# Block-causal attention and a two-layer product on one core: batch 0's second half in float32, two chunks of 192 to a bank, identity inside the plan, and work that may go to more than one engine

## The chip, the cores and the metric

The kernel runs on one core of a Trainium2 chip. The core has a matrix engine (TensorE, PE in the profile; PEld are its weight loads), a vector engine (DVE), an activation engine (ACT), a general engine (GpSimd, POOL) and a queue that issues transfers (SyncE, SP). The metric is the device time of one execution in microseconds, as the median of several runs. Before the change it is 1071.83 us (three runs, 1071.18 to 1075.56).

## What is computed

`q`, `k` and `v` are 8 batches x 8 heads x 576 positions x 64, in float32. Each head does softmax attention in which a block of 64 positions sees itself and the blocks before it. The heads' outputs, put side by side, are 4608 rows of 512, and these go through two products with `h * tanh(softplus(h))` (Mish) between them:

```python
scores = scale * np.matmul(q, k.transpose(0, 1, 3, 2))
mask = block_i >= block_j
scores = np.where(mask, scores, -1000000000.0)
scores = scores - np.max(scores, axis=-1, keepdims=True)
attn = np.exp(scores)
attn = attn / (np.sum(attn, axis=-1, keepdims=True) + 1e-09)
...
h = x @ w_in            # 512 x 2048
g = h * np.tanh(sp)     # sp is softplus(h)
return (g @ w_out)      # 2048 x 512
```

The weights reach the kernel as 64-bit words, which it turns into float32 itself.

## The kernel before

**Numbers.** A float32 value is scaled by a power of two and held as two float16 parts, high and low; a product is then three float16 products (high-high, high-low, low-high). Where the kernel calls a pair of heads "own" or "wide", it skips the split and multiplies float32 as it is.

**Units of work.** A batch has four pairs of heads and two halves of its queries: `HALVES` are positions 0 to 384 and 384 to 576. A `Tile` is one half of one batch; it has 384 or 192 columns.

- `load_pair` (line 733) brings a pair's queries and keys in. Own pairs (batch 0, half 0) read float32 straight into buffers laid over `Et` (`firsts`, lines 351 to 367). All others load into the single tiles `ql` and `kl`, square and sum them (line 811, ACT), reduce across partitions on POOL (line 819), work out scales on DVE (lines 451, 461 and 824), round to the high part `xh` (line 842 on ACT or 849 on DVE), take the remainder `xl` (line 857, DVE), and copy the parts crosswise into a set `QA`, `QB`, `KA`, `KB` by twelve transfers (line 876). There are two such sets. The first nine pairs (`WIDE = 9`) keep the values `V` in float32; later ones split them (lines 892 to 903).
- `attend` (line 934) does one head and one half: the score product A (line 954, from `KA` and `QA`) into one of two PSUM tiles `ss`; the column maximum over key chunks (lines 979 and 992, into `mt`); its maximum over partitions by an all-reduce on POOL (line 1021, into `mr`); minus that maximum into a row of `QB` (line 1028 on DVE or 1035 on ACT); the second score product B (line 954 again, from `KB` and `QB`), which adds the row and the low-order part; the exponential (line 1046, ACT, needs a table); a memset on POOL that hides masked blocks (line 1057); high and low parts of the result (lines 1064 or 1069, and 1075); the value product `u` (line 1092 in float32; 1103 to 1105 as three float16 products); the division by the sum (lines 1126 to 1152); and its two halves `xt_hi` (1163 or 1168) and `xt_lo` (1171). There is one PSUM tile for `u`.
- `weight` (line 489) turns one quarter of a weight matrix into float32 (lines 528 and 545, DVE), sums its squares (556, ACT; 564, POOL), rounds it to the high part (578 on ACT or 585 on DVE) and makes the low part, for three quarters of `w_in` on PE with a scaled identity (596 to 619).
- `Tile.turn` (1194) transposes `xt_hi` and `xt_lo` by transfers; `m1` (1217) is the first product with the Mish activation (1262, ACT, another table than the exponential's); `split` (1278) makes high and low parts of the result; `m2` (1316) is the second product, its evacuation (1357 or 1364) and the store. `m1` and `m2` use a ring of three PSUM tiles `acc`.

**The order.** Nothing is issued as it is written. Each step is put into a `Plan` (line 122) with its engine, an estimated time, what it comes after, and the rings of buffers it takes and frees. `Plan.order` (251) runs a small simulation of the five queues, forward and backward in turns (`go`, line 160), from due times in the table `DUE`; each simulated engine that is free takes the ready step with the earliest due time. The order of the best round is emitted, and each engine executes its own list in that order. A step given with `other=` may run on a second engine, and the simulation takes the one that is free:

```python
for e in o.ways:
    ready[e].append((due[i], i))
```

Steps that are outside the plan come first: memsets, mostly on POOL (lines 350 to 442), and the identity (line 478, on POOL) with its negative (479, on ACT).

Of the kernel before, what the change touches and what calls it, by code (L numbers as in the profile page):

```python
# [19 lines left out]
P = 128  # L20
D = 64
EPS = 1e-9
# [7 lines left out]
    "w": ((198, 45.5, 93.5, 196.5), (118, 220.5, 212.5, 283)),  # L30
    "batch": (209, 220, 278.5, 419.5, 570, 584.5, 680, 822.5),
    "load": (
        (68, 178.5, 94, 89.5),
        (30.5, 24, 165.5, 75.5),
        (143, 130.5, 114.5, 381.5),
        (249, 231.5, 537, 626),
        (450, 465, 506, 532),
        (588, 502.5, 635.5, 628.5),
        (601, 778.5, 735, 673.5),
        (770, 742, 753.5, 656.5),  # L40
        (1259, 954, 806.5, 722.5),
    ),
    "tile": (
        (-10, 235, 68, 43, 118, 37, 41.5, 27.5,
         62.5, 140, 114, 81, 57, 122, 242.5,
         124, 242.5, 120, 204.5, 123.5, 192, 191.5),
        (183.5, 167.5, 87, 61, 129, 80.5, 91, 168.5,
         187.5, 187.5, 115, 163, 265.5, 268.5, 150,
         152, 228.5, 207, 210, 253, 206, 251),
        (103, 130, 155, 132.5, 215, 161, 223.5, 254,  # L50
         188, 203, 201, 270, 399.5, 239.5, 212,
         236, 333.5, 253, 340.5, 375.5, 275.5, 297),
        (253, 168.5, 125.5, 198.5, 289.5, 223, 331.5, 201.5,
         270.5, 394, 316, 368, 286, 369, 296.5,
         511, 308, 562.5, 417.5, 301.5, 373.5, 497.5),
        (232, 318.5, 267, 318, 322.5, 342.5, 487, 377.5,
         415.5, 371.5, 407.5, 319.5, 372.5, 377, 435,
         367.5, 415.5, 399.5, 433, 405.5, 368, 381),
        (328.5, 234, 438.5, 423, 666.5, 634.5, 798.5, 750.5,
         354, 429, 449.5, 442.5, 669.5, 602.5, 621,  # L60
         451.5, 411, 455.5, 533, 469, 648, 604.5),
        (474, 527, 530.5, 473, 536.5, 440, 425.5, 417.5,
         444, 541, 539.5, 524, 546.5, 716, 589,
         645, 449, 529.5, 520, 558, 710, 554),
        (380.5, 532.5, 342.5, 384, 451.5, 504.5, 630.5, 609,
         554, 495.5, 586.5, 512, 660.5, 538, 660.5,
         526, 612.5, 544.5, 692.5, 752.5, 760.5, 719),
        (481, 516, 610, 701.5, 676, 702, 588, 666.5,
         622, 748.5, 705, 739.5, 812.5, 655.5, 692,
         758, 790.5, 750.5, 855, 753.5, 751.5, 828.5),  # L70
        (683.5, 611.5, 574, 555.5, 764.5, 884.5, 506.5, 776,
         585, 615, 733.5, 611.5, 700.5, 680, 625,
         723, 945.5, 630.5, 737, 824, 666, 700),
        (585, 586, 612, 666.5, 620, 811.5, 578, 809,
         599.5, 541, 612.5, 626.5, 682.5, 781, 569.5,
         668.5, 655, 724.5, 657.5, 594.5, 814, 665),
        (781, 620.5, 638, 598.5, 699, 685, 692, 535,
         744.5, 796, 710, 762, 990.5, 631.5, 568,
         884, 869.5, 886, 735.5, 917, 1007, 823),
        (638.5, 1084.5, 660.5, 1071.5, 884, 798.5, 888.5, 766.5,  # L80
         586.5, 780.5, 618, 585, 843.5, 643.5, 933.5,
         766, 646.5, 875, 595, 775.5, 807, 983),
        (736.5, 605, 640.5, 609.5, 734.5, 726.5, 837, 818.5,
         882.5, 881, 857.5, 741, 963, 902, 1124.5,
         1161.5, 996, 738, 735, 794, 766, 751.5),
        (797, 835, 1111, 713.5, 806, 783.5, 943, 780.5,
         868.5, 936, 874.5, 882.5, 849.5, 863, 1069.5,
         1038, 1039, 975.5, 930, 958, 1087.5, 817.5),
        (779, 851, 790, 618.5, 759.5, 896, 933, 783,
         853, 997.5, 1080, 949, 1101, 1129, 1002.5,  # L90
         1131.5, 1065, 950, 955, 943, 989.5, 784.5),
# [30 lines left out]
class Plan:  # L122
# [7 lines left out]
    LAT, LATPE, OWN = 0.15, 0.2, 0.06  # L130
# [10 lines left out]

    def part(self, kind, *at):
# [5 lines left out]
    def add(self, eng, us, emit, after=(), take=(), free=(), other=None, table=None):  # L148
        self.ops.append(Op(eng, us, emit, after, take, free, self.due, other))
        self.ops[-1].table = table  # L150
        return self.ops[-1]

    def lat(self, a, b):
        if a.eng == "sp":
            return self.BEGIN + a.work + self.DONE
        if a.eng != b.eng or len(a.ways) > 1 or len(b.ways) > 1:
            return self.LATPE if a.eng == "pe" else self.LAT
        return 0.0 if a.eng == "pe" else self.OWN

    def go(self, due, back=False):  # L160
# [14 lines left out]
        while events:  # L175
            now = events[0][0]
            while events and events[0][0] <= now:
# [11 lines left out]
                for x in getattr(o, after):  # L189
                    j = x.i  # L190
                    lat = self.lat(x, o) if back else self.lat(o, x) * (o.eng != "sp")
# [59 lines left out]
    def order(self):  # L251
# [6 lines left out]
        _, end, _ = self.go([o.due for o in ops])  # L258
        best = None
        for _ in range(self.ROUNDS):  # L260
# [23 lines left out]
def products(ns, full=False, rows=128):  # L284

    if full:
        return sum(n / 600 + 0.07 - min(n, 320) / 9000 for n in ns), sum(n * rows / 32 for n in ns)
# [11 lines left out]
def pool(n):  # L299
    return 0.4 + n / 230  # L300
# [8 lines left out]
def attention_moe(  # L309
# [44 lines left out]
    for i in range(NP):  # L354
# [8 lines left out]
        nc.gpsimd.memset(m["KF"][D:P, 0], 0.0)  # L363
        nc.gpsimd.memset(m["KF"][0:D, 1], 0.0)
        for j in (0, P + 1):
            nc.gpsimd.memset(m["VF"][:, :, j : j + 1], 1.0)
        firsts.append(m)
    sets = []
    for i in range(2):
        shapes = {  # L370
            "QA": [P, 2, S],
            "QB": [D + 1, 2, S],
            "KA": [P, 2, KW],
# [5 lines left out]
        for nm, t in (  # L379
# [7 lines left out]
        nc.gpsimd.memset(m["KB"][0:D, :, S:KW], 0.0)  # L387
        for j in (0, P + 1):
            nc.gpsimd.memset(m["VF"][:, :, j : j + 1], 1.0)
        nc.gpsimd.memset(m["VF"][64:P, 4, 1 : 1 + P], 0.0)  # L390
# [26 lines left out]
    dv, tt = room(2, "dv", [P, 6]), room(2, "tt", [P, 3, D])  # L417
    ql, kl = room(1, "ql", [P, S])[0], room(1, "kl", [P, S])[0]
# [22 lines left out]
    for t in pe[1], p_hi[1], p_lo[1]:  # L441
        nc.gpsimd.memset(t[:, 896:1024], 0.0)
# [26 lines left out]


# [7 lines left out]
    make_identity(nc, ident)  # L478
    nc.scalar.mul(minus, ident, -1.0)
# [9 lines left out]
    def weight(which, wait, room_free):  # L489
# [11 lines left out]
        last = [None] * len(raws)  # L501
        done = []
        for g in range(NG):
# [6 lines left out]
            for r in range(0, nrow, per):  # L510
# [12 lines left out]
                    [last[i]] + wait,  # L523
# [26 lines left out]
                last[i] = a  # L550
# [31 lines left out]
                other=(  # L582
# [5 lines left out]
                ),  # L588
            )
            if g < PEW[which]:  # L590
# [8 lines left out]
                    [sc] + scaled[-2],  # L599
# [52 lines left out]
    def batch(b):  # L652
# [38 lines left out]
        new["sx"] = add("dve", 0.6, scale_x, [red])  # L691

# [36 lines left out]
    WIDE = 9  # L729
# [762 lines left out]
```

## Time and profile before

| | |
|---|---|
| median of three runs | 1071.83 us |
| the profiled execution | 1073.09 us |
| its span, first to last instruction | 1071.3 us |
| mean granted TensorE clock | 0.971 |
| matmul records of lines 1237 and 1331 (`m1` and `m2`) | 6144 of 9958 |
| activation tables changed | 173 times, 1283 ns each |
| all-reduces of the maximum on POOL | 128, mean 1567 ns |

A group's row has its line, engine, operation, what it writes and reads, shapes and count; then busy time in microseconds and the mean of one in nanoseconds; then the idle time of that engine just before, and what ended it. In a timeline the first number is the start in microseconds and the second the duration; a bracket at the end has the idle time before it. "issue" as the cause of a wait means that the profile shows nothing that the engine waited for. A row of waits has the total in microseconds, how many times, and the longest. Matmuls are pipelined, so their recorded durations overlap: what one costs is read from the distance between starts. Some matmul records can be missing.

### The profile page before, as it was taken

The numbers are of one execution on the slowest core, as the hardware profiler recorded it, in microseconds if no ns is written. First come the engines' busy times: TensorE is split into PE (matmuls) and PEld (weight loads), VectorE is DVE, ScalarE is ACT, GpSimd is POOL, SyncE is SP. The second block draws the span as 40 slices with busy tenths as digits, with TensorE's granted clock in tenths as the row PEclk, the third lists the DMA queues.
The fourth block names the chain that finished last, engine by engine and source line by source line (L and its number), as shares of the span: only waits on it lengthen the run. The fifth ranks groups of instructions, "written<-read, shape, count | busy, mean of one in ns | idle before, by whom it ended". The sixth has DMA issues, their size and how long they took to land. (4 is left out here: it accounts for less than half of the span.)

```text
span 1071.3 us, 25657 instructions
## 1 busy us (share of the span) xinstructions
PE 1009.7 (94%) x9958; PEld 766.2 (72%) x9958; DVE 739.8 (69%) x1872; ACT 771.2 (72%) x1239; POOL 268.7 (25%) x410
## 2 busy tenths in 40 slices
PE   2888989989999999999999999999999998999998
PEld 1466767777776687777767687677778686767778
DVE  3888888785987578757885678746887578833500
ACT  2557887766988679867877789758887688735521
POOL 4242332241232033312431122212332133301000
PEclk7867999999999999999999999999999999999999
DMA  7767643342434433340435233441434342220100
GB/s 253 215 208 185 198 119 86 95 111 77 98 78 110 107 72 77 106 110 25 105 100 128 64 74 96 113 102 28 105 91 110 91 94 71 50 45 8 31 15 23
DMA packets 126200, 103.78 MB, mean 97 GB/s; under 512 B 51328, under 2 KB 112256, under 8 KB 126080
## 3 DMA queue, kind: packets, MB, share of 16 engines
q1 hardware_dynamic: 126080, 102.16, 36.5%
q8 instruction: 78, 1.28, 0.5%
q14 instruction: 42, 0.34, 0.1%
HBM read 56.10 MB, written 9.44 MB: 61 GB/s over the span
## 5 line engine op out<-in xcount | busy, mean ns | idle before, releaser
L1331 PE MATMUL acc<-Gt,wo_h 128*128 128x192 f16 (+1 forms) x2048 | 385.8, 287 | 1.9 <-ACT Et L1262 1.1
L1237 PE MATMUL acc<-x_lo,wi_h 128*128 128x192 f16 (+1 forms) x1024 | 295.0, 288 | 3.2 <-DMA x_lo<-xt_lo 3.2
L1237 PE MATMUL acc<-x_hi,wi_h 128*128 128x192 f16 (+1 forms) x1024 | 295.1, 288 | 2.0 <-ACT Et L1262 1.3
L1237 PE MATMUL acc<-x_hi,wi_l 128*128 128x192 f16 (+1 forms) x1024 | 295.0, 288 | 0.0
L1331 PE MATMUL acc<-Gt,wo_l 128*128 128x192 f16 (+1 forms) x1024 | 293.8, 287 | 0.0
L1021 POOL PARTITION_ALL_REDUCE mr<-mt x128 | 199.6, 1567 | 300.9 <-DVE mt L992 265.6
L1237 PEld LDWEIGHTS <-wi_h 128*128 128x128 f16 x2048 | 192.2, 98 | 77.4 <-issue 10.6
L1331 PEld LDWEIGHTS <-wo_h 128*128 128x128 f16 x2048 | 188.2, 98 | 51.2 <-issue 1.8
L1262 ACT ACTIVATE Et<-acc,bv 128x384 f32<-128x384 f32 (+1 forms) x256 | 125.5, 498 | 91.0 <-PE acc L1237 89.1
L992 DVE TENSOR_TENSOR mt<-mt,ss 128x192 f32<-128x192 f32 (+3 forms) x448 | 127.6, 297 | 13.6 <-ACT mt L979 9.2
L1304 DVE SCALAR_TENSOR_TENSOR Gt<-Et,bv,Gt 128x1536 f16<-128x1536 f32 (+1 forms) x64 | 91.5, 1431 | 54.2 <-ACT Gt L1291 54.0
L1331 PEld LDWEIGHTS <-wo_l 128*128 128x128 f16 x1024 | 100.0, 98 | 34.5 <-issue 1.3
L1237 PEld LDWEIGHTS <-wi_l 128*128 128x128 f16 x1024 | 100.4, 98 | 33.7 <-issue 1.2
L1046 ACT ACT_TABLE_LOAD x86 | 110.3, 1283 | 18.6 <-PE ss L954 8.2
L1046 ACT ACTIVATE pe<-ss,pv 128x768 f32<-128x768 f32 (+1 forms) x120 | 113.2, 956 | 7.9 <-PE ss L954 5.4
L1075 DVE TENSOR_TENSOR p_lo<-pe,p_hi 128x768 f16<-128x768 f32 (+1 forms) x108 | 113.4, 1051 | 4.5 <-ACT p_hi L1064 3.5
L1057 POOL MEMSET pe<- 64x64 f32 (+1 forms) x192 | 34.4, 210 | 318.1 <-ACT pe L1046 287.1
L1262 ACT ACT_TABLE_LOAD x87 | 111.6, 1283 | 1.5
L954 PE MATMUL ss<-QB,KB 65*128 65x192 f16 (+5 forms) x512 | 67.0, 254 | 29.9 <-POOL pv L819 13.0
L1103 PE MATMUL u<-V,p_hi 128*128 128x65 f16 x810 | 85.4, 194 | 2.1 <-DVE tt L1152 2.1
L1105 PE MATMUL u<-V,p_lo 128*128 128x65 f16 x810 | 84.7, 194 | 0.8 <-DVE p_lo L1075 0.6
L1104 PE MATMUL u<-V,p_hi 128*128 128x64 f16 x810 | 85.3, 193 | 0.0
(107 smaller groups left out, 1391.0 us busy)
## 6 DMA issues: line engine op xcount, KB each, us to landing
VL<-in_v_dram SPq DMA_DIRECT2D x32, 288.0 KB, 3.3
kl<-in_k_dram SPq DMA_DIRECT2D x32, 288.0 KB, 3.2
wo_l<-in_w_in_dram SPq DMA_DIRECT2D x8, 1024.0 KB, 5.7
Gt<-in_w_out_dram SPq DMA_DIRECT2D x16, 512.0 KB, 4.0
ql<-in_q_dram SPq DMA_DIRECT2D x28, 288.0 KB, 3.4
QA<-xh SPq DMA_DIRECT2D x112, 72.0 KB, 2.2
VL<-in_v_dram SPq DMA_DIRECT2D x27, 256.0 KB, 3.0
out_dram<-ot SPq DMA_DIRECT2D x32, 192.0 KB, 2.1
```

Source lines behind the costliest of these rows:

```text
L954: nc.tensor.matmul(ss[:, col : col + q1 - qs], lhsT=k_, rhs=q_, start=x == 0 and col % 512 == 0, stop=True, skip_group_check=True,)
L992: nc.vector.tensor_max(t, t, sv(ss_[A.slot % NSS]))
L1021: lambda: nc.gpsimd.partition_all_reduce(mr[rm][:, 0:n], mt[rm][:, 0:n], P, RED.max),
L1046: lambda: nc.scalar.activation(*spread(pe[rm], ss_[A.slot % NSS]), AF.Exp, scale=st.get("esc", D ** -0.5)),
L1075: lambda: nc.vector.tensor_sub(p_lo[rm][:, 0:W], pe[rm][:, 0:W], p_hi[rm][:, 0:W]),
L1103: nc.tensor.matmul(o, lhsT=h, rhs=vh, start=j == 0 and z == 0, stop=False)
L1104: nc.tensor.matmul(o[:, 0:D], lhsT=h, rhs=vo, start=False, stop=False)
L1105: nc.tensor.matmul(o, lhsT=l, rhs=vh, start=False, stop=end)
L1237: nc.tensor.matmul(pt[:, 0:n], lhsT=w[:, d, f * P : (f + 1) * P], rhs=x[:, d, :], start=d == 0 and z == 0, stop=d == NP - 1 and z == 2,)
L1262: nc.scalar.activation(Et[:, (self.i * NG + g) % NE, j, 0:n], acc_[c.slot % NACC][:, 0:n], AF.Mish, scale=fc[:, 0, g : g + 1])
L1304: lambda g_hi=g_hi, g_lo=g_lo, ev=ev: nc.vector.scalar_tensor_tensor(out=g_lo, in0=ev, scalar=self.s_g, in1=g_hi, op0=ALU.mult, op1=ALU.su ...
L1331: nc.tensor.matmul(pt[:, 0:n], lhsT=w[:, f, o * P : (o + 1) * P], rhs=g, start=f == 0 and z == 0, stop=f == NF - 1 and z == 2,)
```

## The change

- **Batch 0's second half.** `ring_pairs(0, Q0, (1,), True)` now loads its pairs as own ones: queries of 384 to 576 into a part of `ql` or `kl`, keys into `KF`, a float32 view over the memory of `QA` and `KA` (now one tile `QK`), with no scales, splits or crossing transfers. The score product A is then float32. `WIDE` is 8: batch 1's first pair splits its values.
- **Chunks of 192 share a bank.** In tiles of 192 columns (`K = 2`) two chunks of `m1` go to the two halves of one `acc` tile, and one Mish activation reads both; in `m2` two output chunks share a tile and a store, with two evacuation instructions.
- **Two heads share a weighing.** The value products of a pair's two heads for one half go to one `u` tile, which is taken by the first head and freed after the second's; sums, reciprocal, weighting, `xt_hi` and `xt_lo` are then done once for both.
- **Identity in the plan.** It follows batch 0's first all-reduce on POOL.
- **Several possible engines.** `other` is a list, and POOL is a third choice for three kinds of step.
- **Memsets** for the own pairs are merged; those of the sets go to DVE.
- **The planner:** new due times throughout, a slack of 0.7 us ahead of PE steps after batch 0, and other cost figures (`OWN`, `pool`, the float32 products of up to 65 columns, the scales, the row of `QB`).

The diff, cut to its core:

```diff
-        if other:
-            self.ways[other[0]] = other[1:]
+        for way in other:
+            self.ways[way[0]] = way[1:]
...
-            return self.LATPE if a.eng == "pe" else self.LAT
+            return self.LATPE if a.eng == "pe" else self.LAT + b.slack
...
 def pool(n):
-    return 0.4 + n / 230
+    return 0.42 + n / 300
+
+
+def elem(n):
+
+    return 0.2 + n / 700
...
-        nc.gpsimd.memset(m["KB"][D : D + 1], MSC)
-        nc.gpsimd.memset(m["KA"][:, :, S:KW], 0.0)
+        nc.vector.memset(m["KB"][D : D + 1], MSC)
+        nc.vector.memset(m["QK"].bitcast(F32), 0.0)
...
-    make_identity(nc, ident)
-    nc.scalar.mul(minus, ident, -1.0)
...
             hi = add(
                 "act",
                 act(2048) + 0.09,
...
+                ), (
+                    "pool",
+                    elem(2048),
+                    lambda whi=whi, f=f, g=g: nc.gpsimd.tensor_scalar_mul(
+                        whi, f, w_s[:, 0, g : g + 1]
+                    ),
+                )],
...
+        if b == 0:
+            e = add("pool", 0.6, lambda: make_identity(nc, ident), [red])
+            last["unit"] = [
+                e,
+                add("act", act(P), lambda: nc.scalar.mul(minus, ident, -1.0), [e]),
+            ]
...
-    WIDE = 9
+    WIDE = 8
...
-                (m["Q"], qT[b, rows, q0:q1], []),
-                (m["KF"][0:D, 0], kT[b, rows, 0:k1][0:D], []),
-                (m["KF"][D:P, 1], kT[b, rows, 0:k1][D:P], []),
+                (m["Q"], qT[b, rows, q0:q1], wait),
+                (m["KF"][0:D, 0, 0:k1], kT[b, rows, 0:k1][0:D], wait),
+                (m["KF"][D:P, 1, 0:k1], kT[b, rows, 0:k1][D:P], wait),
...
+                ), (
+                    "pool",
+                    elem(n),
+                    lambda j=j, n=n, src=src: nc.gpsimd.tensor_scalar_mul(
+                        xh[j][:, 0:n], src, sc[:, j : j + 1]
+                    ),
+                )],
...
-            [p_in] + st["C"],
-            take=[u_ring],
-        )
+            [p_in] + st["C"] + st["u", half],
+            take=[] if a else [u_ring],
+        )
...
-            lambda: nc.scalar.copy(th, tx),
-            [o] + old,
...
+                ("pool", elem(nqc * P), lambda: nc.gpsimd.tensor_copy(out=th, in_=tx)),
...
+                    Et[:, (self.i * NG + g) % NE, j : j + K, 0:n],
+                    acc_[c.slot % NACC][:, 0 : K * n].rearrange("p (k n) -> p k n", k=K),
...
-    ring_pairs(0, Q0, (1,))
+    ring_pairs(0, Q0, (1,), True)
...
+        plan.slack = SLACK
```

More of the change, by code (lines that the diff above doesn't have):

```diff
@@ L21 @@
 D = 64
+E = D + 1
 EPS = 1e-9
@@ L56 @@
[L56 to L67, printed above, removed]
@@ L146, in part, with add @@
             self.due = self.due[i]
-    def add(self, eng, us, emit, after=(), take=(), free=(), other=None, table=None):
+    def add(self, eng, us, emit, after=(), take=(), free=(), other=(), table=None):
         self.ops.append(Op(eng, us, emit, after, take, free, self.due, other))
         self.ops[-1].table = table
+        self.ops[-1].slack = self.slack * (eng == "pe")
         return self.ops[-1]
@@ L190, in go @@
                     j = x.i
-                    lat = self.lat(x, o) if back else self.lat(o, x) * (o.eng != "sp")
+                    lat = self.lat(x, o) if back else self.lat(o, x)
+                    if o.eng == "sp" and not back:
+                        lat = x.slack
                     at[j] = max(at[j], now + lat)
@@ L257, in order @@
                 o.due = min(o.due, n.due - o.us - self.lat(o, n))
-        _, end, _ = self.go([o.due for o in ops])
+        start, end, engine = self.go([o.due for o in ops])
         best = None
+        if None not in engine:
+            best = max(end), start, end, engine
         for _ in range(self.ROUNDS):
@@ L522, in weight @@
                     ),
-                    [last[i]] + wait,
+                    [used[i]] + wait,
                 )
@@ L1371, in m2, with evac, evac_act @@
-                ev_ = self.evacs
+                ev_ = self.evacs
+                def evac(op, o=o, c=parts[0], e=o // K):
+                    for k in range(K):
+                        cols = slice(k * n, (k + 1) * n)
+                        op(
+                            ot[ev_[e].slot % 2][:, cols],
+                            acc_[c.slot % NACC][:, cols],
+                            fc[:, 1, o + k : o + k + 1],
+                        )
+                def evac_act(evac=evac):
+                    evac(lambda o, i, s: nc.scalar.activation(o, i, AF.Copy, scale=s))
```

460 lines of the change are left out of this document (245 added, 215 removed).

## The prediction

> **What bounds the kernel now.** I read the page's busy shares first, then the busy time by stretches of 25 us, then who waited for whom, then the opening 40 us engine by engine.
>
> ```profile
> span 1071.3 us, 25657 instructions
> ...
> PE 1009.7 (94%) x9958; PEld 766.2 (72%) x9958; DVE 739.8 (69%) x1872; ACT 771.2 (72%) x1239; POOL 268.7 (25%) x410
> ```
>
> ```profile
> 0.00:25.00 25.00, 5.29 (x12) 3.38 (x12) 8.75 (x16) 6.01 (x13) 10.53 (x42) 0.81 0.73 243
> 25.00:50.00 25.00, 21.85 (x69) 11.84 (x69) 22.04 (x49) 14.22 (x31) 9.75 (x15) 0.78 0.67 213
> ...
> 100.00:125.00 25.00, 24.16 (x168) 17.42 (x169) 22.60 (x65) 20.72 (x34) 7.12 (x9) 0.91 0.72 209
> ...
> 275.00:300.00 25.00, 23.99 (x240) 17.53 (x239) 22.37 (x55) 23.16 (x38) 8.90 (x12) 1.00 0.40 96
> ```
>
> The columns after the length are PE, weight loads, DVE, ACT, POOL, the granted clock, DMA share and GB/s. There are two stages. Up to about 100 us PE mostly waits or does little of the product work: 5.3 us in the first 25, and a granted clock of 0.78 in the next. There the vector engine (DVE) is full (22.04 of 25). After that PE sets the pace, 24 of 25 us and more, and after 180 us it loses little; its two longest waits there, in total, times and longest:
>
> ```profile
> PE ss L954 <- ACT QB L1035: 9.3, 10, 1.6
> PE acc L1237 <- DMA x_lo<-xt_lo: 3.2, 5, 0.9
> ```
>
> The first is the second score product waiting for the row of negative maxima (QB), which comes from POOL's all-reduce. So from here on a microsecond that the maximum comes late beyond its slack is a microsecond of PE, because each engine's order is fixed when the program is made.
>
> **The opening.** POOL, ACT and PE in the first 26 us, with the two places where POOL changed its code:
>
> ```profile
> 17.16 0.28 POOL masks.py:199 TENSOR_SCALAR_AFFINE_SELECT p_lo<-p_lo 128x128 f32<-128x128 f32 x1 [7.19 <-issue]
> 23.46 1.44 POOL L1021 PARTITION_ALL_REDUCE mr<-mt  x1 [6.02 <-DVE mt L992]
> ...
> 25.22 1.50 POOL L1021 PARTITION_ALL_REDUCE mr<-mt  x1
> ```
>
> ```profile
> masks.py:199 POOLq MODIFY_POOL_CONFIG  x2: 21/21/21, 10.0 to 10.0; - x2
> ```
>
> ```profile
> L1021 POOLq MODIFY_POOL_CONFIG  x2: 1/1/1, 17.7 to 17.7; - x2
> ```
>
> ```profile
> 20.40 0.27 DVE L992 TENSOR_TENSOR mt<-mt,ss 64x128 f32<-64x128 f32 x1
> ```
>
> ```profile
> 17.48 0.31 ACT L479 ACTIVATE p_lo<-p_lo 128x128 f16<-128x128 f32 x1 [15.46 <-POOL p_lo masks.py:199]
> ```
>
> ```profile
> 25.44 0.80 PE L954 MATMUL ss<-QB,KB 1*128 1x256 f16 x3 [13.03 <-POOL pv L819]
> ```
>
> The select that builds the identity had nothing to wait for, and still POOL was idle for 7.19 us, from a configuration instruction at 10.0 us on. The first all-reduce has its input at 20.67 us (DVE's 20.40 plus 0.27) but starts at 23.46, 6.0 us after the select; a configuration again stands at the head of that gap. The next all-reduce follows without any. I read this as POOL running one set of code at a time: memset needs none, the select got one, the all-reduce another, and each change costs 6.0 to 7.2 us in which POOL does nothing.
>
> The Trainium skill says in its "GPSIMD Engine Reference", section 2.1 "Instruction dispatch", that POOL's kernels are loaded at run time and that the first call to a freshly loaded one pays about 6 us (5.95) that no instruction shows; 6.02 and 7.19 agree with it. It does not say which operations share a set.
>
> **The change, part by part.**
>
> *Identity moved behind the first all-reduce, memsets merged or given to DVE.* ACT no longer stands for 15.46 us before its first copy. One load of all-reduce code remains. PE's 13.03 us wait could shrink by up to about 12, but from 25 us on DVE is full, so the stage gets back only what DVE could not do meanwhile: it ran 8.75 of the first 25 us. The added DVE memsets fit in that idle time; without it they would cost about 4 us, from what POOL needs for the same clearing. If the select needs its own code again, up to 13.2 us go back to the stage. I take -7 (from +1 to -12).
>
> *Batch 0's second half in float32.* It removes for four pairs two squares on ACT, a small all-reduce, the scale arithmetic, two roundings, two remainders on DVE, and twelve crossing DMAs each on SP's queue; loads go straight into the pair sets.
>
> ```profile
> L857 DVE SCALAR_TENSOR_TENSOR xl<-kl,pv,xh 128x576 f16<-128x576 f32 x32 | 25.9, 808 | 0.1
> ```
>
> ```profile
> 25.37 0.77 DVE L451 TENSOR_SCALAR pv<-pv 128x2 int32<-128x2 int32 x1
> ```
>
> With 0.81 for that remainder, half of it for the shorter query one (192 columns, an estimate) and 0.77 for the first step of the scales, DVE saves at least 2.0 us a pair, 8 us in all, in a stage where it is 88 to 90% busy (22.04 and 22.60 of 25). Half of that shows: -4 (0 to -11, since roundings and further steps are left out). PE gets more work instead:
>
> ```profile
> 40.06 1.47 PE L954 MATMUL ss<-Et 128*128 128x256 f32 x6
> ```
>
> ```profile
> 85.28 0.52 PE L954 MATMUL ss<-QA,KA 128*128 128x192 f16 x5
> 85.64 2.15 PE L1092 MATMUL u<-V,pe 128*128 128x65 f32 x18
> ```
>
> ```profile
> 302.06 0.19 PE L1103 MATMUL u<-V,p_hi 128*128 128x65 f16 x1
> ...
> 302.57 0.19 PE L1105 MATMUL u<-V,p_lo 128*128 128x65 f16 x1
> ```
>
> A float32 score of 768 columns takes 1.47 us, so one of 832 takes 1.59 against 0.52 in float16: +1.07 for eight heads, +8.6. Batch 1's first pair (WIDE 9 to 8) goes the other way. A float32 value product of 9 blocks takes 2.15 us; split into halves, eighteen products start within 0.54 us, so 27 need 0.81. With 6 blocks it is two thirds of that. Two heads save 2 x (1.34 + 0.89) = 4.5. PE is the bound by then: net +4.1 (0 to +8.6).
>
> *Chunks of 192 share a bank, two heads share one weighing.*
>
> ```profile
> L1262 ACT ACTIVATE Et<-acc,bv 128x384 f32<-128x384 f32 x128 | 72.7, 579 | 57.2 <-PE acc L1237 56.4
> ...
> L1262 ACT ACTIVATE Et<-acc,bv 128x192 f32<-128x192 f32 x128 | 52.8, 418 | 33.8 <-PE acc L1237 32.7
> ```
>
> 128 activations of 418 ns become 64 of 579: 16.4 us off ACT. The weighing loses half its small instructions. PE's columns do not change, so this only buys lateness: out of the 9.3 and 3.2 us of PE waits above, -5 (0 to -12).
>
> *Slack of 0.7 us and new due times.* They change the order alone; no row prices them. I take 0 (-10 to +10).
>
> Together -7 - 4 + 4.1 - 5 = -11.9.
>
> *Several possible engines.* POOL may now scale `xh` (56 operations after batch 0, a tensor-scalar), scale the weights' high parts (8, a tensor-scalar), and copy `xt_hi` (a plain copy). The planner hands such work to whichever engine is free, at a cost of 0.2 + n/700 and no cost for a change of code. How it shared two-way work so far:
>
> ```profile
> L849 DVE TENSOR_SCALAR xh<-kl,pv x18: 504/515/605, 26.9 to 917.6; 128x576 f16<-128x576 f32 x18
> ```
>
> ```profile
> L842 ACT ACTIVATE xh<-kl,pv x14: 762/776/782, 87.0 to 861.8; 128x576 f16<-128x576 f32 x14
> ```
>
> 18 to 14: about evenly. With POOL idle 75% of the time, and ACT and DVE both taken in a stretch like 275 to 300 us, a third is a low guess: 19 + 3 = 22 operations, some back to back, so about 20 trips from all-reduce code to tensor-scalar code and back. No tensor-scalar on POOL is in this trace. Its bounds are the two kinds that are: memset (no change of code) and select (a change of 7.19, and 6.02 back). By its name and its work (a scalar operation on a tensor) it is nearest to the select, so I take the change. A round trip then holds POOL for 13.2 us. Part is covered by POOL's own idle time:
>
> ```profile
> POOL pe L1057 <- ACT pe L1046: 287.1, 99, 12.5
> POOL mr L1021 <- DVE mt L992: 265.6, 81, 38.6
> ```
>
> One such gap before a memset is 2.9 us and one before an all-reduce 3.3, so 6.2 are hidden. Queued behind the change of code on POOL are the memset that hides the masked blocks (the two halves of the probabilities wait for it) and the next maximum (QB, the second score product, and behind that all of PE). The slack there, in one instance:
>
> ```profile
> 309.61 0.35 DVE L1028 TENSOR_SCALAR QB<-mr 1x384 f16<-1x384 f32 x1
> 309.99 0.56 DVE L1069 CAST p_hi<-pe 128x768 f16<-128x768 f32 x1
> ...
> 310.67 0.95 DVE L1075 TENSOR_TENSOR p_lo<-pe,p_hi 128x768 f16<-128x768 f32 x1
> ```
>
> ```profile
> 311.66 0.49 PE L954 MATMUL ss<-QB,KB 65*128 65x256 f16 x3
> ```
>
> QB ended at 309.96 and PE used it at 311.66: 1.7 us. So a trip costs PE 13.2 - 6.2 - 1.7 = 5.3 (0 if no code changes, 13.2 with no cover), and twenty cost 106. The copies of `xt_hi` I price at 0: they hang on no product for many microseconds.
>
> By the Trainium skill's 5.95 us a load, the trip would cost 11.9 - 6.2 - 1.7 = 4.0, an estimate, and the forecast below would be 1140.
>
> **The sum.** The profiled execution took 1073.1 us (span 1071.3, and 1.8 around it); the median of the runs is 1.3 lower. 1073.1 - 11.9 + 106 - 1.3 = 1166.
>
> **Rivals.**
>
> 1. *POOL's code does not change, or the planner leaves it no tensor-scalar* (faster; the part about several engines then does nothing). For: 802 us of POOL are idle, and a tensor-scalar may share the all-reduce's code; no row excludes it. Against: two of the three kinds seen needed their own. It decides as soon as a trip is free: 1073.1 - 11.9 - 1.3 = 1060, between 1040 and 1068. Chance 0.30.
> 2. *Nothing covers the trips*: the loads fall between a maximum and its use each time. 20 x 13.2 = 264, so 1324. For: several POOL gaps are near 0 (the all-reduce at 25.22). Against: the mean gaps above. Chance 0.08.
> 3. *The value bank is held over two heads.* A pair's two heads now fill one PSUM tile, of which there is one, so the other half's heads wait until both are weighed. If rounding and remainder of the second head (0.56 + 0.95) stand open in each of 56 pair-halves, 85 us: 1060 + 85 = 1145, with POOL free of changes. Against: PE has product work between. Chance 0.05.
> 4. *Only the opening pays*: POOL changes code once there and back, 13.2, and the gains cover it: 1060 + 13 = 1073. Chance 0.05.
>
> The forecast itself has 0.52. Its own range: 12 to 24 trips at 3 to 9 us give 36 to 216, so 1096 to 1276. The whole range reaches down to the faster case, 1046 to 1276; some 0.06 lie below and 0.11 above. Half a percent, 5 us, is about what can be told from no change: faster 0.30 (rival 1), the same 0.05 (rival 4), slower 0.65 (the rest).
>
> **What would show it.** Tensor-scalars on POOL, each with idle time of 6 to 7 us and a configuration instruction ahead of it, and the same ahead of the next all-reduce; PE's waits for QB rising from 9.3 to about 100 us; the first second-score product near 14 us instead of 25.44; ACT's 192-column activations gone. I am wrong if POOL shows tensor-scalars with no such gaps, or none at all; then the time is near 1060.

## The result and the profile after

The changed kernel takes **1273.62 us** (median of four runs, 1273.07 to 1280.65) against 1072.55 for the kernel before beside it: a ratio of 1.1885, with an interval of 1.1836 to 1.1934. That is 201 us slower, and 108 us more than the 1166 forecast. The profiled execution took 1274.14 us.

The page of the changed kernel, with the span, the busy times and the granted clock in 40 slices:

```profile
span 1272.1 us, 25351 instructions
...
PE 1054.7 (83%) x10028; PEld 797.0 (63%) x10028; DVE 696.0 (55%) x1587; ACT 724.1 (57%) x1050; POOL 312.2 (25%) x433
...
PEclk7779698988897899999998899989999898989999
```

Before, PE was busy for 94% of the span; now it stands for 217 us (1272.1 less 1054.7; it was 62). DVE and ACT have fewer instructions and less work than before, and all three big engines are idle for longer: none of them became the bound. The clock, which before stayed at 9 in all but four slices, is below 9 in sixteen. The row before:

```profile
PEclk7867999999999999999999999999999999999999
```

What POOL does, by groups (line, operation, shapes and count; busy time and mean of one in ns; idle time before):

```profile
L881 POOL TENSOR_SCALAR xh<-kl,pv 128x576 f16<-128x576 f32 x11 | 19.0, 1729 | 79.0 <-issue 49.9 <-ACT Et L1318 14.6 <-ACT Gt L1350 7.3
L881 POOL TENSOR_SCALAR xh<-ql,pv 128x576 f16<-128x576 f32 x11 | 19.0, 1728 | 71.5 <-DMA kl<-in_k_dram 35.4 <-issue 28.8 <-DVE dv L1202 7.2
L1220 POOL CAST xt_hi<-tt 128x384 f16<-128x384 f32 (+1 forms) x29 | 17.1, 591 | 22.9 <-DVE tt L1203 22.2 <-DVE pv L470 0.3
L610 POOL TENSOR_SCALAR wi_h<-wo_h,wi_s 128x2048 f16<-128x2048 f32 x1 | 5.4, 5445 | 7.8 <-issue 7.8
```

There are 22 roundings of `xh` and two of the weights (one of them shown). All but one, which follows another directly, have about 7 us of idle time ahead of them: 79.0 over 11, 71.5 over 10, 7.8 for one. The 29 plain copies of `xt_hi` have 0.8 us, all of it spent on their input. The configuration marks, two to a change of code, stand ahead of line 881 and of line 1057, the all-reduce of the maximum:

```profile
L881 POOLq MODIFY_POOL_CONFIG  x42: 4/85/88, 161.8 to 1103.1; - x42
```

```profile
L1057 POOLq MODIFY_POOL_CONFIG  x44: 1/2/15, 4.2 to 1112.8; - x44
```

With those of the weights and of the small all-reduces that is 47 pairs of marks: 23 ahead of tensor-scalars and 24 ahead of all-reduces. The first all-reduce's pair belongs to no trip: its gap of 7.25 us ends with its input, which DVE finishes at 11.22 us (the all-reduce starts at 11.41). So there are **23 round trips**. The idle time is 7.2 us there and 6.15 us back by the median (7.22 and 6.53 by the mean, in which one gap of 14.09 us also holds a wait for ACT): some 13.4 us a trip without any work. One of them, on POOL's timeline:

```profile
272.69 0.68 POOL L845 PARTITION_ALL_REDUCE pv<-pv  x1 [0.93 <-ACT xl L837]
280.19 1.73 POOL L881 TENSOR_SCALAR xh<-ql,pv 128x576 f16<-128x576 f32 x1 [6.82 <-DMA kl<-in_k_dram]
288.46 1.44 POOL L1057 PARTITION_ALL_REDUCE mr<-mt  x1 [6.54 <-issue]
```

The same moment on ACT and on PE:

```profile
289.93 0.52 ACT L1071 ACTIVATE QB<-mr 1x384 f16<-1x384 f32 x1 [11.23 <-POOL mr L1057]
```

```profile
279.56 0.33 PE L1394 MATMUL acc<-Gt,wo_h 128*128 128x192 f16 x2
...
279.81 0.33 PE L1394 MATMUL acc<-Gt,wo_h 128*128 128x192 f16 x2
...
290.50 0.80 PE L987 MATMUL ss<-QB,KB 65*128 65x256 f16 x3 [10.29 <-ACT QB L1071]
291.09 0.53 PE L1394 MATMUL acc<-Gt,wo_h 128*128 128x192 f16 x2
...
291.57 0.53 PE L1394 MATMUL acc<-Gt,wo_h 128*128 128x192 f16 x2
```

POOL is away from 273.37 to 288.46. The maximum whose all-reduce comes next is late, ACT waits 11.23 us with the row of QB at the head of its list, and PE stands for 10.29 us with a second score product at the head of its own. The last lines show a second price: a group of three products of 192 columns starts every 0.25 us before the stall (279.56 to 279.81) and every 0.48 us after it (291.09 to 291.57). By stretches of 5 us (PE, weight loads, DVE, ACT, POOL, granted clock):

```profile
275.00:280.00 5.00, 5.00 (x79) 4.03 (x77) 2.34 (x6) 3.66 (x5) 0.00 (x0) 1.00 0.22 62
280.00:285.00 5.00, 0.22 (x3) 0.07 (x1) 0.82 (x1) 0.00 (x0) 1.73 (x1) 0.99 0.19 53
285.00:290.00 5.00, 0.00 (x0) 0.00 (x0) 0.07 (x1) 0.07 (x1) 1.49 (x2) 0.50 0.01 6
290.00:295.00 5.00, 4.50 (x46) 4.15 (x46) 4.20 (x9) 4.70 (x7) 2.21 (x3) 0.50 0.33 98
295.00:300.00 5.00, 5.00 (x76) 4.91 (x74) 3.92 (x11) 2.62 (x5) 1.80 (x7) 0.99 0.48 124
```

The clock falls to 0.50 while PE stands, and stays there until about 295: 4.5 us of work at half speed, which costs 2.3 us after the wait itself is over. The Trainium skill says this in "TensorE: Matmul & The Clock Gate", Part 1: an idle window of about 3.4 us halves the clock, and about as much sustained work releases it. This trace shows the same with somewhat longer times: in stretches of half a microsecond the clock is still 1.00 at 284.5, 4.3 us after PE's last product ended, and 0.50 from 285 on, and it is back at about 295, 4.5 us after work resumed.

Over the whole kernel, who waited for whom (total, times, longest):

```profile
ACT QB L1071 <- POOL mr L1057: 167.9, 44, 16.3
...
POOL mr L1057 <- issue: 110.8, 18, 6.8
DVE xl L889 <- POOL xh L881: 106.3, 19, 7.1
PE ss L987 <- ACT QB L1071: 96.0, 13, 15.2
...
PE ss L987 <- DVE QB L1064: 47.8, 15, 10.8
```

PE's waits for QB are 143.8 us now. Over all of the kernel before they were:

```profile
PE ss L954 <- ACT QB L1035: 11.5, 11, 2.2
...
PE ss L954 <- DVE QB L1028: 5.0, 8, 1.2
```

### The profile page after: what moved, and what is told of

Same layout as the page of the kernel before. It is cut to its first block, busy times and chain, and to the rows that moved or that the text cites. A ratio compares the mean times of both kernels' runs of the same rounds, so it can differ in the third digit from the quotient of the medians.

```text
span 1272.1 us, 25351 instructions
## 1 busy us (share of the span) xinstructions
PE 1054.7 (83%) x10028; PEld 797.0 (63%) x10028; DVE 696.0 (55%) x1587; ACT 724.1 (57%) x1050; POOL 312.2 (25%) x433
## 4 chain that ended last, share of the span: by engine, by line
PE 44%; issue 11%; DVE 8%; ACT 8%; POOL 6%; DMA 3%; SPq 2%; ACTq 0%; DVEq 0%; POOLq 0%
PE acc L1394 19%; PE acc L1292 17%; PE ss L987 4%; PE u L1130 4%; POOL mr L1057 3%; POOL xh L881 2%; ACT L1082 2%; ACT pe L1082 2%; DVE mt L1028 1%; ACT L1318 1%; DMA VL<-in_v_dram 1%; DMA kl<-in_k_dram 1%; DVE p_lo L1111 1%; SPq L1259 1%; ACT Et L1318 1%
## 5 line engine op out<-in xcount | busy, mean ns | idle before, releaser
L1394 PE MATMUL acc<-Gt,wo_h 128*128 128x192 f16 (+1 forms) x2048 | 397.1, 291 | 0.0
L1057 POOL PARTITION_ALL_REDUCE mr<-mt x128 | 185.1, 1453 | 372.3 <-DVE mt L1028 219.1
L987 PE MATMUL ss<-QB,KB 65*128 65x192 f16 (+7 forms) x512 | 71.8, 267 | 144.0 <-ACT QB L1071 96.0
L1318 ACT ACTIVATE Et<-acc,bv 128x384 f32<-128x384 f32 x192 | 109.7, 578 | 87.6 <-PE acc L1292 86.4
L987 PEld LDWEIGHTS <-KB 65*128 65x128 f16 (+1 forms) x512 | 44.1, 101 | 163.8 <-issue 149.7
L1111 DVE TENSOR_TENSOR p_lo<-pe,p_hi 128x896 f16<-128x896 f32 (+1 forms) x112 | 115.1, 1029 | 32.9 <-ACT p_hi L1100 31.0
L1082 ACT ACTIVATE pe<-ss,pv 128x896 f32<-128x896 f32 (+1 forms) x112 | 106.0, 953 | 42.3 <-PE ss L987 21.9
L1071 ACT ACTIVATE QB<-mr 1x384 f16<-1x384 f32 (+1 forms) x68 | 30.3, 446 | 168.7 <-POOL mr L1057 167.9
L1130 PE MATMUL u<-V,p_hi 128*128 128x65 f16 (+1 forms) x1680 | 98.0, 198 | 24.9 <-DVE tt L1203 11.9
L1130 PEld LDWEIGHTS <-p_hi 128*128 128x128 f16 x1680 | 92.8, 101 | 36.4 <-DVE tt L1203 13.5
```

Of the source, the lines that this page charges most:

```text
L987: nc.tensor.matmul(ss[:, col : col + q1 - qs], lhsT=k_, rhs=q_, start=x == 0 and col % 512 == 0, stop=True, skip_group_check=True,)
L1057: lambda: nc.gpsimd.partition_all_reduce(mr[rm][:, 0:n], mt[rm][:, 0:n], P, RED.max),
L1071: lambda: nc.scalar.mul(m["QB"][D : D + 1, a, q0:q1], mr[rm][D : D + 1, 0:n], -1.0 / MSC),
L1082: lambda: nc.scalar.activation(*spread(pe[rm], ss_[A.slot % NSS]), AF.Exp, scale=st.get("esc", D ** -0.5)),
L1111: lambda: nc.vector.tensor_sub(p_lo[rm][:, 0:W], pe[rm][:, 0:W], p_hi[rm][:, 0:W]),
L1130: nc.tensor.matmul(o, lhsT=l, rhs=r, start=start, stop=stop, skip_group_check=True)
```

## The experiments

Each kernel ran beside the kernel before on the same chip (medians of before there lay between 1070.6 and 1073.3). "Rest" is the span less PE's busy time, both from the page of the profiled execution. A round trip ("trip") is a change to the tensor-scalar's code and back. The kernels did not all run on the same chip, and before differs by up to 2.7 us between the chips and rounds, so a difference of that size between two rows says nothing by itself; the ratios are the safer comparison.

| kernel | trips | median us | ratio to before, interval | span | PE busy | rest | clock |
|---|---|---|---|---|---|---|---|
| before | 0 | 1072.55 | | 1071.3 | 1009.7 | 61.6 | 0.971 |
| changed | 23 | 1273.62 | 1.1885 (1.1836 to 1.1934) | 1272.1 | 1054.7 | 217.4 | 0.906 |
| order kept, on DVE | 0 | 1050.65 | 0.980 (0.9767 to 0.9833) | 1046.3 | 998.4 | 47.9 | 0.986 |
| order kept, plain copies on POOL | 0 | 1050.3 | 0.9793 (0.9751 to 0.9834) | 1048.3 | 1003.6 | 44.7 | 0.983 |
| order kept, every second one on DVE | 12 | 1157.33 | 1.0791 (1.0756 to 1.0826) | 1156.9 | 1029.1 | 127.8 | 0.939 |
| order kept, on DVE, empty trips | 23 | 1227.33 | 1.1444 (1.1418 to 1.1471) | 1227.2 | 1046.4 | 180.8 | 0.921 |
| before, with tensor-scalars on POOL | 30 | 1385.07 | 1.2914 (1.2859 to 1.2969) | 1382.8 | 1085.2 | 297.6 | 0.868 |
| no tensor-scalar on POOL, planned anew | 0 | 1056.29 | 0.9856 (0.982 to 0.9891) | 1054.9 | 1013.2 | 41.7 | 0.969 |
| the same, second half in float16 | 0 | 1057.87 | 0.9867 (0.9846 to 0.9888) | 1056.5 | 1002.6 | 53.9 | 0.969 |
| the same, no POOL copies of `xt_hi` | 0 | 1056.44 | 0.9839 (0.981 to 0.9867) | 1055.8 | 1010.0 | 45.8 | 0.976 |
| the same, `p_hi` on POOL too | 0 | 1077.89 | 1.0038 (1.0025 to 1.005) | 1077.4 | 1020.6 | 56.8 | 0.962 |
| the same, slack 0 | 0 | 1069.81 | 0.9971 (0.9955 to 0.9987) | 1068.1 | 1011.6 | 56.5 | 0.974 |
| the same, one chunk a bank | 0 | 1129.69 | 1.052 (1.0504 to 1.0536) | 1126.1 | 1032.7 | 93.4 | 0.939 |
| before, identity in the plan | 0 | 1070.71 | 0.9985 (0.9971 to 0.9999) | 1066.3 | 1005.8 | 60.5 | 0.974 |

### The order kept, the tensor-scalars on DVE

The planner makes the order of the changed kernel, with its own estimates; only then the steps that it had put on POOL are emitted for DVE, in their places. Order, buffers and arithmetic are otherwise those of the changed kernel.

```diff
             o.us, o.emit = o.ways[e]
+            if e == "pool" and getattr(o, "ts", False):
+                o.emit = o.ways["dve"][1]
```

> The changed kernel with its plan and the order on every engine kept; only the 24 tensor-scalars that the plan gave to POOL are issued on DVE, at the same places. If POOL's changes of code cost the time: about 1060 us (1040 to 1085), no configuration on POOL but the first, PE's waits for QB near 10 us in place of 144. If the new plan (due times, slack, the value bank held over two heads) costs it: 1220 or more.

Measured: 1050.65 us, with one pair of configuration marks in the whole kernel, at the start. PE's waits for QB, by the view of waits, are 19.3 us, more than the 10 expected:

```profile
PE ss L991 <- DVE QB L1068: 10.1, 8, 5.5
PE ss L991 <- ACT QB L1075: 9.2, 4, 3.8
```

24 operations in another place are worth 223 us (1273.62 less 1050.65), so everything else in the change together is a gain of 20 to 22 (against the runs of before beside it, or beside the changed kernel). The span shrinks by 225.8 us, of which 169.5 are PE's standing (217.4 less 47.9) and 56.3 are PE's busy time (1054.7 less 998.4), for the same count of products. That these 56.3 are nearly all the clock can be worked out: PE's busy time in slices of 2.5 us, each times the clock granted in it, adds up to 989.5 us in the changed kernel and to 988.1 here. Over 23 trips: **7.4 of standing and 2.4 of slower work, 9.8 a trip** by the spans of the two profiled executions (9.7 by the medians). This kernel computes all that the changed one does, and is faster than both.

### The same 24 steps on POOL, as plain copies

```diff
-                    lambda j=j, n=n, src=src: nc.gpsimd.tensor_scalar_mul(
-                        xh[j][:, 0:n], src, sc[:, j : j + 1]
+                    lambda j=j, n=n, src=src: nc.gpsimd.tensor_copy(
+                        out=xh[j][:, 0:n], in_=src
```

> The changed kernel with its plan kept; the 24 operations stay on POOL with the same sizes, as plain copies that need no code of their own. The scaling is left out, so what follows computes on unscaled high parts. If the changes of code cost the time: within 20 us of the run before it. If POOL being slow at this work (1.73 us each where the plan had 1.02), or the late high parts, costs it: 1200 or more.

Measured: 1050.3 us. The copies leave out the scaling, so this kernel does not compute the same thing. POOL's group of one of them:

```profile
L879 POOL CAST xh<-kl 128x576 f16<-128x576 f32 x11 | 8.0, 729 | 0.0
```

The work is on the same engine, in the same place of its list, of the same size, and has no idle time ahead of it. So it is not that POOL has these steps in its queue or that their results come from there: the price hangs on which operation it is. A plain copy also takes 729 ns for the 576 columns that the tensor-scalar does in 1729.

### Half of the trips

```diff
+            if e == "pool" and getattr(o, "ts", False):
+                moved += 1
+                if moved % 2:
+                    o.emit = o.ways["dve"][1]
```

> The changed kernel with its plan kept; every second of the 24 tensor-scalars goes to DVE, 12 stay on POOL. If each trip costs on its own, about half of the 223 us between the changed kernel and the one with none stays: 1160 us (1140 to 1180). If a few trips at bad places make most of it, it lies outside that.

Measured: 1157.33 us, with 12 trips: 106.7 us above the kernel with none, 8.9 a trip against 9.7 (223 over 23). The price is close to linear.

### Empty trips

All 24 steps run on DVE, and where each stood on POOL there is a multiplication of one column that nothing reads:

```diff
+    def both(emit):
+        def op():
+            emit()
+            nc.gpsimd.tensor_scalar_mul(spare[:, 0:1], spare[:, 1:2], 1.0)
+        return op
```

> The changed kernel with its plan kept; the 24 real tensor-scalars on DVE, and in their place on POOL one of a single element each, on which nothing waits. If it is POOL being held by its change of code that costs, nearly all of it stays: 1230 to 1270 us. If it is the high parts coming late (DVE's remainders waited 106 us for them), most goes: under 1130.

Measured: 1227.33 us, a little under the range that the theory gave. POOL's group:

```profile
L473 POOL TENSOR_SCALAR spare<-spare 128x1 f32<-128x1 f32 x24 | 6.8, 282 | 163.4 <-issue 120.3 <-ACT VL L714 14.1 <-DVE wo_l L674 7.6
```

6.8 us of work that nobody waits for cost 176.7 us (1227.33 less 1050.65), 79% of the 223. By the table PE stands 132.9 us longer than without trips and is busy 48.0 longer: 5.8 and 2.1 a trip. What is left of the 223, 46 us or 2.0 a trip, comes with the real operations: they take 1.73 us each (5.4 for weights), and their high parts come late (DVE's 106.3 us of waits above). Which of the two counts was not separated.

### The kernel before, with only the tensor-scalars allowed on POOL

```diff
+                    elem(n),
+                    lambda j=j, n=n, src=src: nc.gpsimd.tensor_scalar_mul(
+                        xh[j][:, 0:n], src, sc[:, j : j + 1]
+                    ),
```

> The kernel before with one thing added: POOL as a third engine for the same two tensor-scalars; its plan puts 32 of them on POOL. Changes of code at the 9 us a trip that the changed kernel suggests, some 28 trips: about 1320 us (1250 to 1380). If the loss needs the other parts of the change: under 1100.

Measured: 1385.07 us, just above the range that was expected. The planner gives POOL 33 tensor-scalars, in 30 trips: 10.4 us a trip (312.5 over 30), though the order is a new one too and its share is not known. One part of the change alone, put into the old kernel, is slower than the whole change. Where the all-reduce comes first and the select behind it, POOL's timeline shows a detail:

```profile
10.16 1.43 POOL L1035 PARTITION_ALL_REDUCE mr<-mt  x1
11.49 0.74 POOL masks.py:199 TENSOR_SCALAR_AFFINE_SELECT p_lo<-p_lo 128x128 f32<-128x128 f32 x1
12.96 1.72 POOL L1035 PARTITION_ALL_REDUCE mr<-mt  x1 [0.73 <-DVE mt L1006]
```

Neither the first all-reduce nor the select behind it has a gap for a change of code. In the kernel before the select came first and paid 7.19 us, and the all-reduce behind it 6.02.

### The change without the tensor-scalars on POOL, planned anew

The two POOL ways with `tensor_scalar_mul` are taken out; all else is the changed kernel's.

```diff
-                ), (
-                    "pool",
-                    elem(n),
-                    lambda j=j, n=n, src=src: nc.gpsimd.tensor_scalar_mul(
-                        xh[j][:, 0:n], src, sc[:, j : j + 1]
-                    ),
```

> The changed kernel without the third engine for the two tensor-scalars, planned anew (the copies of xt_hi may still go to POOL). Changes of code: about 1060 us (1040 to 1080). Another cause: 1200 or more.

Measured: 1056.29 us. This is the base for five of the next six. It lies 5.6 us above the first kernel, which differs only in the order and in how ACT and DVE share the roundings (26 and 30 of `xh` here, 15 and 41 there): so much a new plan alone can do.

### Batch 0's second half as before

```diff
-    WIDE = 8
+    WIDE = 9
...
-    ring_pairs(0, Q0, (1,), True)
+    ring_pairs(0, Q0, (1,))
```

> The changed kernel without POOL's tensor-scalars and with batch 0's second half split into float16 again (nine wide pairs), planned anew. By the prediction's two terms (DVE -4, PE +4.1) it takes the same time as with float32, 1056 within 5 us. If the removed work on DVE, ACT and SP weighs more: 1062 or more. If the longer PE work does: 1051 or less.

Measured: 1057.87 us, 1.6 from the base, with intervals that overlap almost wholly. PE's busy time shows the exchange: 1013.2 us with float32, 1002.6 without, and the rest 41.7 against 53.9. What PE gains by waiting less, it pays back in work: multiplied by the clock, as above, its busy time is 986.3 against 981.0, so 5.3 of the 10.6 are longer products (4.1 was forecast) and the rest is a lower clock.

### The identity behind the first all-reduce, alone

```diff
-    make_identity(nc, ident)
-    nc.scalar.mul(minus, ident, -1.0)
...
+        if b == 0:
+            e = add("pool", 0.6, lambda: make_identity(nc, ident), [red])
```

> The kernel before with the identity made behind the first all-reduce on POOL and nothing else. By the prediction's step: 7 us less than before (from +1 to -12), one change of code on POOL in place of two. If the opening is bound by DVE and the weights' transfers alone: no difference (within 3 us).

Measured: 1070.71 us over ten runs against 1072.62 over thirteen, a gain of 1.9 (ratio 0.9985, 0.9971 to 0.9999). That is the other outcome that was named, no difference within 3 us. Both changes of code are gone, not one of two: the first all-reduce starts right behind its marks, and the select later pays nothing either.

```profile
L1025 POOLq MODIFY_POOL_CONFIG  x2: 21/21/21, 9.8 to 9.9; - x2
```

```profile
9.96 1.61 POOL L1025 PARTITION_ALL_REDUCE mr<-mt  x1
```

Its first stretches:

```profile
0.00:25.00 25.00, 15.44 (x45) 10.03 (x45) 15.99 (x36) 11.77 (x21) 16.05 (x47) 0.80 0.90 306
25.00:50.00 25.00, 12.72 (x48) 8.28 (x49) 17.61 (x50) 12.40 (x26) 6.33 (x12) 0.59 0.80 245
...
25.00:30.00 5.00, 3.20 (x9) 1.66 (x10) 4.93 (x10) 1.32 (x3) 2.00 (x3) 0.60 0.78 208
30.00:35.00 5.00, 0.08 (x1) 0.07 (x1) 4.87 (x10) 2.67 (x4) 2.44 (x2) 0.50 0.23 40
35.00:40.00 5.00, 0.71 (x3) 0.17 (x2) 0.85 (x8) 3.68 (x7) 1.16 (x4) 0.50 0.90 260
```

PE does 15.44 us of work in the first 25 where it did 5.29, and DVE 15.99 where it did 8.75. But in the next 25 PE does 12.72 where it did 21.85: the head start is given back at once. From 25 to 35 us DVE is full (4.93 and 4.87 of 5) and PE falls to 0.08 of 5; from 35 to 40 both mostly stand, while the transfers are at 0.90, and the clock is at 0.50. That DVE and then the transfers hold this stage is read from these rows and was not tested.

### No POOL copies of `xt_hi`

```diff
-                ("pool", elem(nqc * P), lambda: nc.gpsimd.tensor_copy(out=th, in_=tx)),
```

> The changed kernel without the third way for all three kinds of step: no tensor-scalars on POOL, and no plain copies of xt_hi there either. Theory: those 29 copies need no change of code and stand on an engine with time to spare, but ACT and DVE have time too, so they carry next to nothing: within 5 of the kernel without the tensor-scalars (1056). Rival: the copies on POOL are what is left of the gain: back at 1066 or more.

Measured: 1056.44 us, 0.2 from the base: no effect of the copies can be seen.

### A plain copy of `p_hi` on POOL as well

```diff
+                ), (
+                    "pool",
+                    elem(W),
+                    lambda: nc.gpsimd.tensor_copy(out=p_hi[rm][:, 0:W], in_=pe[rm][:, 0:W]),
```

> The changed kernel without the two tensor-scalars on POOL, but with a plain copy on POOL as a third way for the high part of the exponentials (an edit that scales nothing). Theory: POOL does plain copies without a change of code, so work may be given to it there at no fixed price; since ACT and DVE are not what sets the pace after 100 us, the time stays within 8 of 1056. Rival A: a plain copy of this form needs code of its own: then some 50 steps pay a trip and the time is over 1300. Rival B: ACT's and DVE's relief is worth something: under 1048.

Measured: 1077.89 us, 21.6 above the base: neither the theory's figure nor a rival's. POOL's group and PE's waits:

```profile
L1097 POOL CAST p_hi<-pe 128x768 f16<-128x768 f32 (+1 forms) x43 | 43.8, 1019 | 9.2 <-PE u L1122 6.8
```

```profile
PE ss L975 <- ACT QB L1059: 16.1, 10, 5.0
PE ss L975 <- ACT pe L1070: 15.9, 11, 3.6
```

43 copies, with no change of code (0.2 us of idle time each), so that theory holds. In the base kernel these two waits are 5.9 and 5.5 us, so PE waits 20.6 us longer for the row of QB and for the exponentials (its standing grows by 15.1 us in all). The copies stand on the engine that makes the maximum, and the order is a new one; which of the two moves the waits was not separated.

### Slack 0

```diff
-    SLACK = 0.7
+    SLACK = 0.0
```

> The changed kernel without the two tensor-scalars on POOL and with a slack of 0.0 in place of 0.7. Theory: the planner's slack keeps PE's steps from being put just behind what they wait for, and carries part of the 16 us by which this kernel beats the one before: 1060 to 1068. Rival: the slack carries nothing (it was put at 0 in the prediction): within 4 of 1056.

Measured: 1069.81 us, 13.5 above the base. PE's two waits named above are 11.6 and 13.3 us in this kernel. It lies just above the theory's range. A new plan alone has moved the time by 5.6 us, and perhaps by more in the run before, so it is not shown that the slack itself is worth 13.5.

### One chunk a bank

```diff
-            self.K = Q0 // self.n
+            self.K = 1
```

> The changed kernel without the two tensor-scalars on POOL and with K = 1: each chunk of 192 has a bank, an activation, an evacuation and a store of its own, as before the change. Theory: of the merges this one carries most, since it halves the activations and the hand-overs of a ring of three: 1062 to 1070. Rival: the merge of two heads' weighing, or the planner, carries the gain: within 4 of 1056.

Measured: 1129.69 us, far above both. Two stretches near the end, of this kernel and then of the base:

```profile
950.00:975.00 25.00, 14.02 (x147) 10.48 (x146) 15.81 (x41) 11.48 (x19) 10.38 (x13) 0.50 0.13 31
975.00:1000.00 25.00, 14.50 (x157) 10.70 (x156) 17.28 (x42) 14.19 (x27) 9.30 (x16) 0.50 0.19 48
```

```profile
950.00:975.00 25.00, 25.00 (x284) 19.93 (x282) 9.76 (x21) 17.82 (x21) 2.36 (x5) 1.00 0.03 9
975.00:1000.00 25.00, 25.00 (x234) 19.05 (x232) 7.50 (x7) 10.47 (x15) 0.00 (x0) 1.00 0.11 25
```

From 800 to 925 us this kernel keeps PE full (over 24.9 of each 25 us). Then DVE and POOL still work on maxima, too few other products are there to fill PE, and the clock falls to 0.50. The due times are those of the change, made for half as many chunks; an order with due times of its own was not tried. So what a bank is worth and what the order costs was not separated.

## Why the prediction was right and where it was wrong

**The direction and the mechanism were right.** POOL acts here as if it held one set of code at a time, the planner does not price the change, and PE pays for it, for the most part through the row of QB. The signs that were named are in the trace: 22 + 2 tensor-scalars (22 forecast), 7.2 us there and 6.15 back by the median (7.19 and 6.02), PE's waits for QB at 143.8 us (about 100), the first second-score product at 13.56 us (14), no more activations of 192 columns.

```profile
13.56 0.50 PE L987 MATMUL ss<-QB,KB 1*128 1x256 f16 x3 [1.41 <-DVE QB L1064]
```

**The step that failed is the price of a trip**, "a trip costs PE 13.2 - 6.2 - 1.7 = 5.3". It is 9.7. The runs take the sum apart:

- *The clock was left out.* The sum ended when PE could start again. PE then works at half speed for a while: 2.4 us a trip, 56 us in all, the largest part of the missing 4.4. The prediction had read a clock of 0.78 off the stage where PE waits, so the row was there; it was used to see that stage, and not as a price of the stalls that the change would make.
- *The operation itself was left out.* The sum had the two changes and not the tensor-scalar between them: 1.73 us, 5.4 for a weight. With it and with the late high parts the standing goes from 5.8 to 7.4 us a trip (changed kernel against empty trips, 169.5 less 132.9 over 23, is 1.6).
- *The changes were priced rightly*: 13.4 us a trip, where 13.2 was said.
- *The cover was right on average, and in part by luck.* In the kernel with empty trips POOL is held for some 13.3 us a trip (7.1 there, 5.9 back by the median, 0.3 of work) and PE stands 5.8 longer, where 5.3 was said: 7.5 are hidden, near the 6.2 + 1.7 of the forecast. No single trip shows this. From the start of a trip's idle time to 6 us after the next all-reduce starts, PE stands for anything from 0.2 to 12.0 us in that kernel, and from 0.6 to 15.4 in the changed one. The forecast had put together two mean gaps and one instance of slack.
- *The count* was near: 23 trips and not 20.

Together: three more trips at 5.3 make 16 us, and 23 trips at 9.7 instead of 5.3 make 101. These 117, less 9 because the rest of the change gains more than forecast (1050.65 with the order kept, against 1060), are the 108 between forecast and result.

**The smaller terms.** The opening was put at -7; the identity's move alone, in the kernel before, is -1.9, and the memsets were not tried alone. The head start was forecast to be cut by a full DVE, and was cut by more, down to almost nothing by 50 us. The load of the all-reduce's code that was to remain there did not show: the first all-reduce started 0.1 us behind its marks. Batch 0's second half was put at -4 + 4.1, and is nothing beyond the noise. The rest, merges with due times and slack, was put at -5 + 0: the change without tensor-scalars on POOL gains 16.3 us (1072.6 less 1056.3; 15.4 by its ratio, whose interval is 11.7 to 19.3). Less 1.9 for the identity and 1.6 for the second half, they carry about 12 or 13 together. How that is shared among them stays open: without slack most of it is gone, with one chunk a bank far more than it is gone, and both runs also move the order.

**The rivals.** The first (no change of code) fell with the marks in the trace; the kernel with plain copies shows what it would have been, 1050 where 1040 to 1068 was said. The second (no cover) is wrong in its mechanism, since about 7.5 us of a trip are hidden on average, though the result lies nearer to its 1324 than to 1166, for the terms left out above. The third (the value bank held over two heads) fell with the first experiment, which has that bank and no loss. The fourth needed one trip, and there are 23.

## What to carry to other kernels

Before work is given to an idle engine, look in the trace for what the engine does between its present operations, and price the switch as an operation of its own: an engine that is 75% idle can still be the one that everything waits for. Price a stall of the matrix engine as the wait plus the slow clock behind it, here 7.4 + 2.4 us. And when a planner makes the order, keep its order and change only what is emitted: that separates an operation's price from the price of a new plan, which here moved the time by 5.6 us where little else differed.

## What the runs showed of the hardware

- On POOL, memsets and plain copies (29, 24 and 43 of them in three kernels) ran between all-reduces without a change of code; tensor-scalars paid some 7 us there and some 6 us back at each switch (medians 7.2 and 6.15 in the changed kernel), not at the first use alone, even when the operation was one column wide (0.28 us).
- What a first use costs depends on the order: the select paid 7.19 us as the first of the two, with 6.02 for the all-reduce after it. With the all-reduce first (started at 9.96, its marks at 9.8 to 9.9) neither paid.
- POOL scaled 576 columns from float32 to float16 in 1.73 us, and copied as many with rounding in 0.73.
- The Trainium skill, in "GPSIMD Engine Reference", section 2.1 "Instruction dispatch", gives 5.95 us for the first call to a freshly loaded kernel. The changes here took 7.2 us one way, which is longer, and 6.15 (5.90 with empty trips) the other by the median, which is near it. They came 46 times in this kernel, once for each switch.
